# Attention units of three tiles: half-zero q and v buffers, k by pairs, and the first join in the sums' banks

## The chip, the cores and the metric

The kernel runs on one core of a Trainium2 chip. The metric is the device time of one execution in microseconds; the comparison of two kernels is made from runs on the same chip.

## What is computed

Sliding-window attention with sink positions, and then a gated feed-forward layer on all tokens.

```python
# q, k, v: (4, 8, 768, 64); n_sink 4, window 128
scores = scale * np.matmul(q, k.transpose(0, 1, 3, 2))
keep = is_sink | in_window
scores = np.where(keep, scores, -1000000000.0)
scores = scores - np.max(scores, axis=-1, keepdims=True)
a = np.exp(scores)
a = a / (np.sum(a, axis=-1, keepdims=True) + 1e-09)
attn = np.matmul(a, v)
# x: attn with heads side by side, (3072, 512)
gate = 1.0 / (1.0 + np.exp(-(x @ w_gate)))
val = x @ w_val
out = gate * val @ w_out          # w_gate, w_val: 512 x 1536; w_out: 1536 x 512
```

The weights come as 64-bit floats, in two 32-bit words each.

## The kernel before

**Attention.** Six tiles of 128 queries stand in a sequence. The table `AT` cuts the first batch into two blocks of three tiles and each of the other three batches into three blocks of two. A *unit* `u` is one head of one block, so units 0 to 15 (the first batch) have three tiles; they are the *plain* units and work in f32 without a split. The later units, of two tiles, split their operands into a rounded part and a rest and use rounded f32 (`fp32r`) products. A unit (`attend`, line 795) loads q, k (both transposed, head dimension on partitions) and v; by tile it makes scores q·k on TensorE (`qk`), masks them and takes the row maximum on VectorE (`top`), and exponentiates on ScalarE (`exp`). Then VectorE inverts the row sums (`guard`), one of POOL, ScalarE and VectorE multiplies (`norm`), TensorE transposes (`turn`), ScalarE copies (`wt`), POOL cuts the copy into two triangles (`split`), and TensorE multiplies by v (`pv`). The sink columns are gathered in `psk`.

**Plain units before.** A head has 64 dimensions. q·k takes 64 partitions of `qkT`: from `u = 4` on (`DUP`) one load brings two heads (k of a pair, q of a pair), and the second head uses the upper half. For `u < 4` each head's q and k are loaded twice, into both halves, so that the product has 128 rows, and the scale is halved. p·v of a plain unit has v as its stationary operand, 64 columns, and writes the lower or upper half of the partitions of the bank `xr`. Scores of `u < 8` go into the banks of the output sums (`OS`, named `o`), which the feed-forward part doesn't use yet; all else goes into three rotating banks `a`.

**Join.** After the eight heads of a block, `join` (line 1046) transposes `psk`, splits it (`sk`), multiplies by `vsp` (the sinks' v, from the load `v_sink`), adds the products to `xr`, and writes the sum in rounded part and rest to `XH` and `XL`. These are the operands of the feed-forward part.

**Feed-forward.** `weights` and `decode` (line 1120) load one of twelve sets of weights (set `f`: 128 columns of `w_gate`, of `w_val`, and 128 rows of `w_out`, each through one of three staging tiles `wst`) and turn the 64-bit words into a rounded part and a rest: ScalarE, VectorE and POOL share the work. For each chunk of three tiles and each `f`, `feed_part` makes 24 *up* products (`m<-XH,wgh` and so on, 384 columns), tanh on ScalarE, the gate factor on VectorE (`th`), a split (`gh`, `gl`), and nine *down* products (`o<-woh,gh`, 512 columns). `GATES` lets set 0 be decoded from `u = 2` on and the others only behind `guard` of `u = 7`.

**The order.** `Plan` holds all operations with a priority and estimates of their duration, and before anything is issued it walks through an event list and writes one fixed order for each engine: TensorE prefers attention (its priority is `u`) and fills up with up and down products; where TensorE would be idle early on, it puts in *fill* products (`m<-ident`). Each engine executes in the written order, and all loads stand in one queue, SyncE's. A tile of a pool is taken when its first operation is placed, and `plan.over` says which tiles lie under which others.

Of the kernel before, what the change touches and what calls it, by code (L numbers as in the profile page):

```python
# [32 lines left out]
DUP = 4  # L33
# [37 lines left out]
BUFS = {}  # L71
# [368 lines left out]
def kernel(  # L440
# [70 lines left out]
    def mac(cols):  # L511
        return max(cols * 13 / 12 / 2.4, 104.5) + 2.5
# [55 lines left out]
    def shared(name, n2, n3):  # L568
# [10 lines left out]
    QK = shared("qkT", 256 + 3 * KW, 384 + 4 * KW)  # L579
# [15 lines left out]
    EV = [  # L595
        WST[1][:, 768:960].rearrange("p (l d) -> p l d", d=D),
        WST[2][:, 6 * KW : 6 * KW + 192].rearrange("p (l d) -> p l d", d=D),
    ]
    early_pool = ExitStack()
    ep = early_pool.enter_context(tc.tile_pool(name="early", bufs=1))  # L600

    class Late:
# [4 lines left out]
        def tile(self, *a, **kw):  # L607
            if self.pool is None:
                early_pool.close()
                self.pool = main.enter_context(tc.tile_pool(name="late", bufs=1))  # L610
            return self.pool.tile(*a, **kw)

    late = Late()
    NQ = 3 * KW + 384
    EQ = [ep.tile([128, NQ], F32, name=f"eq{i}") for i in range(3)]
    for tag, n in (("qs", 2), ("kh", 4), ("vhl", 3)):
        for i in range(n):
            plan.over[tag, i] = {("eQ", 0), ("eQ", 1), ("eQ", 2)}
    EW = [WST[1][:, 0:768].rearrange("p (z t y x) -> p z t y x", z=1, t=3, y=2)]
    plan.over["wst", 1] = {("eW", 0), ("eV", 0)}  # L620
    plan.over["wst", 2] = {("eP", 0), ("eP", 1), ("eV", 1)}
# [146 lines left out]
    def load(u, b, h, t0, T, prev, L, vraw, qkT, plain):  # L768
# [20 lines left out]
        dma(  # L789
            u, 182.0 * L, lambda: Q.dma_start(  # L790
                out=vraw(), in_=v[b, h, :, t0 - prev : t0 - prev + L]
            ), w=[vraw],
        )

    def attend(u, b, h, t0, T, XR, XS, PSK, QKT):
# [11 lines left out]
        if early and u % 2:  # L807
            vraw = Tile(EV, None, F32, "eV", 2)
        else:
            vraw = tile([128, L, D], F32, "vraw", BUFS["vraw"])  # L810
        twice = u < DUP
        if not (plain and h % 2 and not twice):
            QKT[0] = (
                Tile(EQ, None, F32, "eQ", 3) if twice and u % 5 > 1 else part(T, QK, "qkT")
            )
        qkT = QKT[0]
        rows = slice(e, e + D) if plain and not twice else slice(0, 128)
        scale = SCALE * (0.5 if twice else 1.0)
        qT = lambda: qkT()[rows, 0:W]
        kTf = lambda: qkT()[rows, W : W + L * KW]  # L820
        load(u, b, h, t0, T, prev, L, vraw, qkT, plain)
        kk2, qq2 = [(qkT, 0), (qkT, 4)], [(qkT, 2), (qkT, 6)]
        if plain:
            pairs = ((qT, kTf),)
            qk_reads = [qkT]
        else:
            qs = tile([128, W], F32R, "qs", 2, late)
            kht = tile([128, 3 * KW], F32R, "kh", 4, late)
            klt = tile([128, 3 * KW], F32R, "kh", 4, late)
# [18 lines left out]
        for t in range(T):  # L848
            sc = Tile(OS, None, F32, "eO", 3) if early else tile([128, 512], F32, "a", BUFS["a"], ps)
# [11 lines left out]
            def top(t=t, sc=sc, first=first):  # L861
                if not first:
                    V.copy_predicated(out=sc()[:, 0:128], mask=tri, data=sc()[:, KW : KW + 128])
                V.tensor_tensor_reduce(
                    out=Pv()[:, t], in0=sc()[:, 0:KW], in1=am[min(t0 + t, 2)], op0=ALU.add,
                    op1=ALU.min, scale=-scale, scalar=3.0e38, accum_out=negm_all[:, at + t : at + t + 1],
                )

            def exp(t=t):
# [6 lines left out]
                u, [("PE", 60 + 2 * n if plain else 20 + 2 * mac(n), qk)], qk_reads, [sc, (P, t)],  # L876
                busy=0.5 if plain and not twice else 0.97,
# [84 lines left out]
        if plain:  # L962
            vhl = vht = vraw
        else:
            vht = tile([128, 3, 2 * D], F32R, "vhl", 3, late)
            vhl = lambda: vht()[:, 0:L]
            copy(u, L * D, lambda: vhl()[:, :, 0:D], vraw, [vraw], [(vht, 0)], L % 2)
            rest(
                u, L * D, lambda: vhl()[:, :, D : 2 * D], vraw, lambda: vhl()[:, :, 0:D],
                [vraw, (vht, 0)], [(vht, 1)],  # L970
            )
# [9 lines left out]
        M = D if plain else 2 * D  # L981
# [189 lines left out]

    def weights(f, prio):
        fs = slice(f * 128, f * 128 + 128)
        wres[f] = []
        for nm, w in (("g", w_gate), ("v", w_val)):
            hi = Fixed(wp.tile([128, NC, 128], F32R, name=f"w{nm}h{f}"))
            lo = Fixed(wp.tile([128, NC, 128], F32R, name=f"w{nm}l{f}"))
            decode(prio(), w[fs], hi, lo)
            wres[f] += [hi, lo]
        hi = Fixed(wp.tile([128, 1, DO], F32R, name=f"woh{f}"))  # L1180
# [8 lines left out]
    def feed(ci, g, parts):  # L1189
# [13 lines left out]
        for j, acc in enumerate(O):  # L1203
            ot = (
                part(2, QK, "qkT") if ci == len(MT) - 1 and j == 2
# [190 lines left out]
```

## Time and profile before

| | us |
|---|---|
| median of 3 runs | 776.95 |
| lowest, highest | 776.75, 776.95 |
| the profiled execution | 776.84 |
| span of the profiled execution, first to last instruction | 775.1 |
| TensorE busy | 761.6 (98%) |
| VectorE busy | 440.0 (57%) |
| ScalarE busy | 413.8 (53%) |
| POOL busy | 385.8 (50%) |

The span is the time between the first and the last instruction; the rest of the execution's time lies around it. Busy shares are means over stages that differ much, so the views below are of stretches. In a timeline a matmul's duration contains the way through the array, and following matmuls overlap; what one costs is read from start to start.

### The profile page before, as it was taken

Reading aid. Unit: us, or ns where it says so; the run is one execution under the profiler, and the core shown is the slowest. Engines: PE = TensorE matmul, PEld = TensorE weight load, DVE = VectorE, ACT = ScalarE, POOL = GpSimd, SP = SyncE. Lnnn points to the kernel's source line nnn. Section 1 sums busy time; section 2 is a strip of 40 time slices with the busy share of each in tenths; the row PEclk is TensorE's granted clock in tenths of the full one; section 3 lists DMA queues with packets and bytes.
Section 4 is the critical chain, followed back from the end, with each engine's and each line's share of the span. In section 5 each row is a group of like instructions: output and inputs, shape, how many; then the busy total and the mean of one; then the engine's idle time right before and its main releaser. Section 6 shows DMA issues by size and latency. Waiting matters only on the chain.

```text
span 775.1 us, 13683 instructions
## 1 busy us (share of the span) xinstructions
PE 761.6 (98%) x4184; PEld 689.9 (89%) x4184; DVE 440.0 (57%) x1398; ACT 413.8 (53%) x1222; POOL 385.8 (50%) x521
## 2 busy tenths in 40 slices
PE   8999999999999999999999999999999999999996
PEld 6577779999999999999999999999999999999995
DVE  5878888978885688938820578836831310100001
ACT  5776778877776676836721586735741321121111
POOL 3567658877786675825721477824731321112110
PEclk9999999999999999999999999999999999999999
DMA  6568788563433443523431235432401211121111
GB/s 174 163 220 279 247 277 261 159 190 109 128 111 103 118 122 100 145 63 124 113 89 44 93 104 147 115 96 85 114 29 49 64 51 42 47 67 59 45 41 59
DMA packets 63444, 90.05 MB, mean 116 GB/s; under 512 B 9220, under 2 KB 40964, under 8 KB 63364
## 3 DMA queue, kind: packets, MB, share of 16 engines
q1 hardware_dynamic: 63360, 89.10, 39.0%
q8 instruction: 35, 0.57, 0.3%
q14 instruction: 45, 0.37, 0.1%
q10 hardware_dynamic: 4, 0.00, 0.0%
HBM read 79.63 MB, written 9.44 MB: 115 GB/s over the span
## 4 chain that ended last, share of the span: by engine, by line
PE 94%; SPq 2%; DVE 1%; DMA 1%; POOL 1%; issue 0%; ACT 0%; DVEq 0%; POOLq 0%
PE m L493 52%; PE o L493 26%; PE a L493 16%; SPq L493 2%; DMA w<-in_v_sink_dram 1%; DVE a L493 0%; DVE P L493 0%; DVE wst L493 0%; POOL vsp L493 0%; POOL kh L493 0%; POOL wst L493 0%; POOL wt L493 0%; DVE gl L493 0%; DVE xr L493 0%; DVE kh L493 0%
## 5 line engine op out<-in xcount | busy, mean ns | idle before, releaser
L493 DVE SCALAR_TENSOR_TENSOR th<-th,m 128x384 f32<-128x384 f32 x96 | 52.9, 552 | 216.9 <-PE m L493 216.5
L493 POOL TENSOR_TENSOR gl<-th,gh 128x384 fp32r<-128x384 f32 x64 | 65.6, 1025 | 213.5 <-ACT gh L493 210.0
L493 PE MATMUL m<-XH,wgh 128*128 128x384 f32 x384 | 132.6, 345 | 0.0
L493 PE MATMUL m<-XH,wvh 128*128 128x384 f32 x384 | 131.4, 342 | 0.0
L493 POOL TENSOR_SCALAR_AFFINE_SELECT wt<-wt 128x512 fp32r<-128x512 f32 (+3 forms) x172 | 107.2, 625 | 46.5 <-DVE wt L493 33.3
L493 PE MATMUL m<-XH,wvl 128*128 128x384 f32 x384 | 129.4, 337 | 0.0
L493 PE MATMUL m<-XL,wvh 128*128 128x384 f32 x384 | 129.1, 336 | 0.0
L493 PE MATMUL m<-XH,wgl 128*128 128x384 f32 x384 | 129.0, 336 | 0.0
L493 PE MATMUL m<-XL,wgh 128*128 128x384 f32 x384 | 128.9, 336 | 0.0
L493 ACT CAST gh<-th 128x384 fp32r<-128x384 f32 x83 | 42.6, 513 | 153.3 <-DVE th L493 153.0
L493 PE MATMUL o<-woh,gh 128*128 128x512 f32 x288 | 117.1, 407 | 0.0
L493 PE MATMUL o<-woh,gl 128*128 128x512 f32 x288 | 113.5, 394 | 0.0
L493 PE MATMUL o<-wol,gh 128*128 128x512 f32 x288 | 112.7, 391 | 0.0
L493 ACT ACTIVATE P<-P,negm_all 128x132 f32<-128x132 f32 x180 | 72.5, 403 | 21.1 <-DVE negm_all L493 19.5
L493 ACT ACTIVATE th<-m 128x384 f32<-128x384 f32 x96 | 46.9, 489 | 67.0 <-PE m L493 66.2
L493 PEld LDWEIGHTS m<-XH,wvh 128*128 128x128 f32 x384 | 72.1, 188 | 4.4 <-issue 1.5
L493 PEld LDWEIGHTS m<-XH,wgh 128*128 128x128 f32 x384 | 72.2, 188 | 3.3 <-issue 2.5
L493 PEld LDWEIGHTS m<-XL,wvh 128*128 128x128 f32 x384 | 72.2, 188 | 2.7
L493 PEld LDWEIGHTS m<-XL,wgh 128*128 128x128 f32 x384 | 72.3, 188 | 0.7
L493 PEld LDWEIGHTS m<-XH,wgl 128*128 128x128 f32 x384 | 72.1, 188 | 0.0
L493 PEld LDWEIGHTS m<-XH,wvl 128*128 128x128 f32 x384 | 72.1, 188 | 0.0
L493 PEld LDWEIGHTS o<-woh,gl 128*128 128x128 f32 x288 | 54.0, 188 | 13.5 <-DVE gl L493 0.3
(135 smaller groups left out, 1445.2 us busy)
## 6 DMA issues: line engine op xcount, KB each, us to landing
wol<-wol_d SPq DMA_DIRECT2D x96, 256.0 KB, 2.7
qkT<-in_k_dram SPq DMA_DIRECT2D x100, 99.0 KB, 2.6
qkT<-in_q_dram SPq DMA_DIRECT2D x144, 64.0 KB, 2.3
wst<-in_moe_w_gate_dram SPq DMA_DIRECT2D x12, 512.0 KB, 4.9
wst<-in_moe_w_val_dram SPq DMA_DIRECT2D x12, 512.0 KB, 3.7
wst<-in_moe_w_out_dram SPq DMA_DIRECT2D x12, 512.0 KB, 4.1
out_dram<-w SPq DMA_DIRECT2D x23, 256.0 KB, 2.1
vraw<-in_v_dram SPq DMA_DIRECT2D x52, 96.0 KB, 2.2
```

Of the source, the lines that this page charges most:

```text
L493: return lambda *a, **kw: tc.keep_in_program_order(op(*a, **kw))
```

## The change

Plain units get buffers that are half zero. `QZ` holds four tiles of 128 partitions: head 0 of a pair has its q in the lower 64 partitions and zeros in the upper ones, head 1 the other way round. `VZ` does the same for v along the columns. k is loaded once by pair, both heads one above the other. q·k then multiplies 128 rows (the other head's k meets zeros), and p·v has 128 columns and writes the whole bank `xr`, where the second head's product is added to the first one's. The zeros are set once, by memsets on POOL and VectorE, since the loads write only the other half. The doubled loads, the halved scale and the early tiles `EQ` and `EV` are gone.

The scores of `u < 10` (`MORE`) instead of `u < 8` go into the sums' banks, and so do the transposes and the four products of the first join, whose priority is moved ahead by 3 (`AHEAD`). The new tiles take the room of the sets `f >= 10` (`LATE`), which are taken when all eight are free; the small tiles of the later units no longer wait for early tiles. The estimates of q·k and p·v in the plan are lower.

```diff
-DUP = 4
+AHEAD = 3.0
+MORE = 10
+LATE = 10
...
-    QK = shared("qkT", 256 + 3 * KW, 384 + 4 * KW)
+    NQ = 256 + 3 * KW
+    raw = const.tile([128, 3 * NQ], F32, name="qkT")
+    QK = [raw[:, i * NQ : i * NQ + NQ] for i in range(3)]
...
+    QZ = [[ep.tile([128, 384], F32, name=f"qz{z}{i}") for i in range(2)] for z in range(2)]
+    VZ = [[ep.tile([128, 4, 128], F32, name=f"vz{z}{i}") for i in range(2)] for z in range(2)]
+    for i in range(2):
+        for z in range(2):
+            nc.gpsimd.memset(QZ[z][i][D - z * D : 2 * D - z * D], 0.0)
+        for z in range(2):
+            nc.vector.memset(VZ[z][i][:, :, D - z * D : 2 * D - z * D], 0.0)
+    EARLY = {(f"{n}{z}", i) for n in ("qz", "vz") for z in range(2) for i in range(2)}
+    for f in range(LATE, NF):
+        for n in ("wgh", "wgl", "wvh", "wvl", "woh"):
+            plan.over[f"{n}{f}_", 0] = set(EARLY)
...
+        e = (h % 2) * D
+        vsrc = v[b, h, :, t0 - prev : t0 - prev + L]
+        if qz:
+            if h % 2 == 0:
+                dma(
+                    u, 1.5 * L * KW, lambda: Q.dma_start(
+                        out=qkT()[:, 0 : L * KW],
+                        in_=k[b, h : h + 2, :, (t0 - prev) * KW : (t0 - prev + L) * KW].rearrange(
+                            "h d n -> (h d) n"
+                        ),
+                    ), w=[qkT],
+                )
+            dma(
+                u, 0.75 * W, lambda: Q.dma_start(
+                    out=qz()[e : e + D, 0:W], in_=q[b, h, :, t0 * 128 : t0 * 128 + W]
+                ), w=[qz],
+            )
+            dma(
+                u, 182.0 * L, lambda: Q.dma_start(out=vt()[:, 0:L, e : e + D], in_=vsrc), w=[vt]
+            )
+            return
...
-            if plain and u >= DUP:
-                if h % 2 == 0:
-                    dma(
-                        u, 1.5 * n, lambda src=src, o=o, n=n, at=at: Q.dma_start(
-                            out=qkT()[:, at : at + n],
-                            in_=src[b, h : h + 2, :, o : o + n].rearrange("h d n -> (h d) n"),
-                        ), w=[(qkT, part)],
-                    )
-                continue
...
         early = u < H
-        if early and u % 2:
-            vraw = Tile(EV, None, F32, "eV", 2)
+        z = h % 2
+        qz = Tile(QZ[z], None, F32, f"qz{z}", 2) if plain else None
+        if plain:
+            vt = Tile(VZ[z], None, F32, f"vz{z}", 2)
         else:
-            vraw = tile([128, L, D], F32, "vraw", BUFS["vraw"])
-        twice = u < DUP
-        if not (plain and h % 2 and not twice):
-            QKT[0] = (
-                Tile(EQ, None, F32, "eQ", 3) if twice and u % 5 > 1 else part(T, QK, "qkT")
-            )
+            vt = tile([128, L, D], F32, "vraw", BUFS["vraw"])
+        vraw = lambda: vt()
+        if not (plain and z):
+            QKT[0] = Tile(QK, None, F32, "qkT", 3)
         qkT = QKT[0]
...
-        rows = slice(e, e + D) if plain and not twice else slice(0, 128)
-        scale = SCALE * (0.5 if twice else 1.0)
-        qT = lambda: qkT()[rows, 0:W]
-        kTf = lambda: qkT()[rows, W : W + L * KW]
-        load(u, b, h, t0, T, prev, L, vraw, qkT, plain)
+        load(u, b, h, t0, T, prev, L, vt, qkT, qz)
         kk2, qq2 = [(qkT, 0), (qkT, 4)], [(qkT, 2), (qkT, 6)]
         if plain:
-            pairs = ((qT, kTf),)
-            qk_reads = [qkT]
+            pairs = ((lambda: qz(), lambda: qkT()[:, 0 : L * KW]),)
+            qk_reads = [qkT, qz]
...
-            sc = Tile(OS, None, F32, "eO", 3) if early else tile([128, 512], F32, "a", BUFS["a"], ps)
+            sc = Tile(OS, None, F32, "eO", 3) if u < MORE else tile([128, 512], F32, "a", BUFS["a"], ps)
...
-                u, [("PE", 60 + 2 * n if plain else 20 + 2 * mac(n), qk)], qk_reads, [sc, (P, t)],
-                busy=0.5 if plain and not twice else 0.97,
+                u, [("PE", (15 + 1.7 * n if plain else 20 + 2 * mac(n)), qk)], qk_reads, [sc, (P, t)],
...
-            a = (xr()[e : e + D] if plain else acc())[:, 0 : Z * W].rearrange("p (z x) -> p z x", z=Z)
+            a = (xr if plain else acc)()[:, 0 : Z * W].rearrange("p (z x) -> p z x", z=Z)
...
-                    start=i == 0, stop=i == len(blocks) - 1, skip_group_check=True,
+                    start=i == 0 and not (plain and z), stop=i == len(blocks) - 1, skip_group_check=True,
...
-                u, [("PE", 60 + sum(2 * n for *_, n in blocks), pv)], [vht, wt], [(xr, h % 2)]
+                u, [("PE", 15 + sum(1.7 * n for *_, n in blocks), pv)], [vht, wt], [xr]
...
-        ts = tile([128, 512], F32, "a", BUFS["a"], ps)
+        first = u == H - 1
+        bank = (
+            lambda: Tile(OS, None, F32, "eO", 3) if first
+            else tile([128, 512], F32, "a", BUFS["a"], ps)
+        )
+        u -= AHEAD if first else 0
+        ts = bank()
...
-                sp = tile([128, 512], F32, "a", BUFS["a"], ps)
+                sp = bank()
...
+    def home(shape, name, f):
+
+        if f < LATE:
+            return Fixed(wp.tile(shape, F32R, name=name))
+        return tile(shape, F32R, name + "_", 1, late)
```

The order changes throughout. SyncE's queue, from the third of the early heads on, before (`w_290<-in_v_sink_dram` is the load for `vsp`, `wst` the staging of weights; `x2` counts equal loads that follow each other):

```order
L493 DMA eq_96<-in_k_dram 64x396 x2
L493 DMA eq_96<-in_q_dram 64x384 x2
L493 DMA vraw_232<-in_v_dram 128x192
L493 DMA eq_97<-in_k_dram 64x396 x2
L493 DMA eq_97<-in_q_dram 64x384 x2
L493 DMA wst_89<-in_v_dram 128x192
L493 DMA qkT<-in_k_dram 128x396
L493 DMA qkT<-in_q_dram 128x384
L493 DMA qkT<-in_k_dram 128x396
L493 DMA qkT<-in_q_dram 128x384
L493 DMA w_290<-in_v_sink_dram 96x512
L493 DMA wst_87<-in_moe_w_gate_dram 128x1024
```

and now:

```order
L495 DMA vz_101<-in_v_dram 128x3x64
L495 DMA qz_99<-in_q_dram 64x384
L495 DMA vz_103<-in_v_dram 128x3x64
L495 DMA qkT<-in_k_dram 128x396
L495 DMA vraw_217<-in_v_dram 128x128
L495 DMA vraw_226<-in_v_dram 128x128
L495 DMA qz_96<-in_q_dram 64x384
L495 DMA qz_98<-in_q_dram 64x384
L495 DMA qkT<-in_k_dram 128x396
L495 DMA vraw_288<-in_v_dram 128x128
L495 DMA w_298<-in_v_sink_dram 96x512
L495 DMA wst_87<-in_moe_w_gate_dram 128x1024
```

The v_sink load has 24 loads ahead of it before and 17 now; among them are now three v loads of later units (`vraw`).

TensorE around the first join, before (`psk` the gathered sinks, `sk,vsp` the join's products, `wt,vraw` p·v of units 8 and 7, `m<-ident` fill):

```order
L493 MATMUL a_568<-ident,psk_277 32x128 x3
L493 MATMUL m_113<-ident 128x128 x3
L493 MATMUL a_582<-wt_547,vraw_444 64x256 x2
L493 MATMUL a_582<-wt_547,vraw_444 64x128 x2
L493 MATMUL a_592<-sk_579,vsp 128x384
L493 MATMUL a_514<-wt_573,wst_89 64x256 x2
L493 MATMUL a_514<-wt_573,wst_89 64x128
L493 MATMUL m_113<-ident 128x128
L493 MATMUL a_609<-sk_579,vsp 128x384
L493 MATMUL m_113<-ident 128x128 x4
L493 MATMUL a_621<-sk_579,vsp 128x384
L493 MATMUL m_113<-ident 128x128
```

and now:

```order
L495 MATMUL o_90<-ident,psk_286 32x128 x3
L495 MATMUL a_573<-ident,wst_89 128x128 x3
L495 MATMUL m_126<-ident 128x128
L495 MATMUL a_586<-wt_556,vz_100 128x256 x2
L495 MATMUL a_586<-wt_556,vz_100 128x128 x2
L495 MATMUL o_91<-sk_581,vsp 128x384
L495 MATMUL o_92<-sk_581,vsp 128x384
L495 MATMUL o_90<-sk_581,vsp 128x384
L495 MATMUL a_604<-qkT,qz_97 128x260
L495 MATMUL o_91<-sk_581,vsp 128x384
L495 MATMUL a_514<-wt_593,vz_103 128x256 x2
L495 MATMUL a_514<-wt_593,vz_103 128x128
```

Before, the four join products stand apart, in banks `a` (the fourth behind the last row shown); now three follow each other in banks `o`, and u=7's transposes and p·v (`a_573`, `a_514`) have come behind the join's own transposes.

TensorE among the up products of set 1, before (`a<-qkT` is a q·k product of a plain unit):

```order
L493 MATMUL m_113<-XH,wgh_122 128x384
L493 MATMUL m_113<-XL,wgh_122 128x384
L493 MATMUL m_113<-XH,wgl_123 128x384
L493 MATMUL a_722<-qkT 128x260
L493 MATMUL a_729<-qkT 128x260
L493 MATMUL m_113<-XH,wgh_122 128x384
L493 MATMUL m_113<-XL,wgh_122 128x384
L493 MATMUL m_113<-XH,wgl_123 128x384
```

and now:

```order
L495 MATMUL a_705<-ident,P 128x128 x3
L495 MATMUL a_713<-qkT,qz_99 128x260
L495 MATMUL m_126<-XH,wgh_135 128x384
L495 MATMUL m_126<-XL,wgh_135 128x384
L495 MATMUL m_126<-XH,wgl_136 128x384
L495 MATMUL m_126<-XH,wgh_135 128x384
L495 MATMUL m_126<-XL,wgh_135 128x384
L495 MATMUL m_126<-XH,wgl_136 128x384
L495 MATMUL a_731<-qkT,qz_99 128x260
L495 MATMUL m_126<-XH,wgh_135 128x384
L495 MATMUL m_126<-XL,wgh_135 128x384
L495 MATMUL m_126<-XH,wgl_136 128x384
```

The two q·k products that stood side by side now stand apart, each between six up products.

## Rows read from the trace of the kernel before

**Rows 1.** The page's part 4: chain that ended last, shares by engine.
```profile
PE 94%; SPq 2%; DVE 1%; DMA 1%; POOL 1%; issue 0%; ACT 0%; DVEq 0%; POOLq 0%
```
**Rows 2.** By stretch: length, busy PE, PEld, DVE, ACT, POOL (instructions); clock, DMA share, GB/s.
```profile
8.20:48.70 40.50, 36.03 (x193) 24.68 (x191) 29.05 (x125) 30.50 (x105) 22.62 (x35) 1.00 0.67 199
48.70:150.00 101.30, 101.30 (x521) 83.42 (x521) 91.01 (x222) 78.66 (x199) 71.17 (x85) 1.00 0.76 244
150.00:768.00 618.00, 617.67 (x3445) 575.57 (x3443) 316.35 (x1032) 302.45 (x919) 290.80 (x390) 1.00 0.32 90
```
**Rows 3.** Timeline of TensorE: start, us, engine, line, operation, out<-in, rows*columns, form, count.
```profile
49.89 0.33 PE L493 MATMUL m<-XH,wvh 128*128 128x384 f32 x1
...
51.80 0.34 PE L493 MATMUL m<-XH,wgl 128*128 128x384 f32 x1
52.06 1.51 PE L493 MATMUL a<-wt,vraw 128*64 128x256 f32 x8
53.51 0.44 PE L493 MATMUL m<-XH,wvh 128*128 128x384 f32 x1
53.79 0.34 PE L493 MATMUL m<-XL,wvh 128*128 128x384 f32 x1
...
55.54 0.34 PE L493 MATMUL m<-XH,wgl 128*128 128x384 f32 x1
55.80 1.14 PE L493 MATMUL a<-qkT 64*128 64x260 f32 x4
56.88 0.44 PE L493 MATMUL m<-XH,wgh 128*128 128x384 f32 x1
57.16 0.34 PE L493 MATMUL m<-XL,wgh 128*128 128x384 f32 x1
...
62.44 0.49 PE L493 MATMUL a<-ident,P 128*128 128x128 f32 x3
62.69 0.42 PE L493 MATMUL m<-XH,wvh 128*128 128x384 f32 x1
62.95 0.34 PE L493 MATMUL m<-XL,wvh 128*128 128x384 f32 x1
```
**Rows 4.** The same timeline: a full-height q·k unit, and a join product between fills.
```profile
7.76 1.27 PE L493 MATMUL o<-qkT 128*128 128x132 f32 x6
8.87 0.38 PE L493 MATMUL m<-ident 128*128 128x128 f32 x2
...
46.08 0.44 PE L493 MATMUL a<-sk,vsp 96*128 96x384 f32 x1
46.37 0.39 PE L493 MATMUL m<-ident 128*128 128x128 f32 x2
```
**Rows 5.** TensorE's groups by shape, 48.7 to 160 us: count | busy us, mean ns | idle.
```profile
L493 PE MATMUL a<-qkT 64*128 64x260 f32 x35 | 10.8, 421 | 0.0
L493 PE MATMUL a<-wt,vraw 128*64 128x256 f32 x28 | 7.5, 392 | 0.0
L493 PE MATMUL a<-wt,vraw 128*64 128x128 f32 x28 | 4.2, 273 | 0.0
```
**Rows 6.** Timeline of TensorE: q·k of two heads together.
```profile
33.38 1.22 PE L493 MATMUL a<-qkT 64*128 64x260 f32 x6
```
**Rows 7.** Timelines of SyncE, VectorE, POOL and TensorE: steps towards the first up product.
```profile
15.09 0.43 SPq L493 DMA_DIRECT2D w<-in_v_sink_dram  x1
19.90 0.42 DVE L493 CAST vsp<-w 96x512 fp32r<-96x512 f32 x1 [0.94 <-DMA w<-in_v_sink_dram]
32.58 0.33 SPq L493 DMA_DIRECT2D wst<-in_moe_w_out_dram  x1
37.74 1.03 POOL L493 TENSOR_TENSOR wst<-wst,rs 128x396 f32<-128x396 f32 x1
48.73 0.44 PE L493 MATMUL m<-XH,wgh 128*128 128x384 f32 x1
```
**Rows 8.** Waits of VectorE and SyncE, 48.7 to 150: us in total, times, longest.
```profile
DVE th L493 <- PE m L493: 3.6, 6, 1.5
DVE P L493 <- PE a L493: 0.9, 1, 0.9
SPq L493 <- PE a L493: 13.3, 7, 4.7
```

More of the change, by code (lines that the diff above doesn't have):

```diff
@@ L594 @@
     EP = [WST[2][:, i * 3 * KW : i * 3 * KW + 3 * KW] for i in range(2)]
[L595 to L598, printed above, removed]
     early_pool = ExitStack()
-    ep = early_pool.enter_context(tc.tile_pool(name="early", bufs=1))
+    ep = early_pool.enter_context(tc.tile_pool(name="early", bufs=1, side="right"))
     class Late:
@@ L609, in tile @@
                 early_pool.close()
-                self.pool = main.enter_context(tc.tile_pool(name="late", bufs=1))
+                self.pool = ctx.enter_context(tc.tile_pool(name="late", bufs=1, side="right"))
             return self.pool.tile(*a, **kw)
     late = Late()
[L614 to L618, printed above, removed]
+    QZ = [[ep.tile([128, 384], F32, name=f"qz{z}{i}") for i in range(2)] for z in range(2)]
[9 more added lines that the diff above has]
+            plan.over[f"{n}{f}_", 0] = set(EARLY)
     EW = [WST[1][:, 0:768].rearrange("p (z t y x) -> p z t y x", z=1, t=3, y=2)]
-    plan.over["wst", 1] = {("eW", 0), ("eV", 0)}
-    plan.over["wst", 2] = {("eP", 0), ("eP", 1), ("eV", 1)}
+    plan.over["wst", 1] = {("eW", 0)}
+    plan.over["wst", 2] = {("eP", 0), ("eP", 1)}
     for i in range(3):
@@ L766, in sinks, with load @@
         )
-    def load(u, b, h, t0, T, prev, L, vraw, qkT, plain):
+    def load(u, b, h, t0, T, prev, L, vt, qkT, qz):
         W = T * 128
+        e = (h % 2) * D
[19 more added lines that the diff above has]
+            return
         for part, src, o, n in ((0, k, (t0 - prev) * KW, L * KW), (2, q, t0 * 128, W)):
             at = 0 if part else W
-            if plain and u >= DUP:
-                if h % 2 == 0:
-                    dma(
-                        u, 1.5 * n, lambda src=src, o=o, n=n, at=at: Q.dma_start(
-                            out=qkT()[:, at : at + n],
-                            in_=src[b, h : h + 2, :, o : o + n].rearrange("h d n -> (h d) n"),
-                        ), w=[(qkT, part)],
-                    )
-                continue
             for i in range(2):
@@ L788, in load @@
                 )
[L789 to L792, printed above, removed]
-        )
+        dma(u, 182.0 * L, lambda: Q.dma_start(out=vt(), in_=vsrc), w=[vt])
     def attend(u, b, h, t0, T, XR, XS, PSK, QKT):
@@ L865, in top @@
                     out=Pv()[:, t], in0=sc()[:, 0:KW], in1=am[min(t0 + t, 2)], op0=ALU.add,
-                    op1=ALU.min, scale=-scale, scalar=3.0e38, accum_out=negm_all[:, at + t : at + t + 1],
+                    op1=ALU.min, scale=-SCALE, scalar=3.0e38, accum_out=negm_all[:, at + t : at + t + 1],
                 )
@@ L962, in attend @@
         if plain:
-            vhl = vht = vraw
+            vhl = vht = vt
         else:
-            vht = tile([128, 3, 2 * D], F32R, "vhl", 3, late)
+            vht = tile([128, 3, 2 * D], F32R, "vhl", 3)
             vhl = lambda: vht()[:, 0:L]
-            copy(u, L * D, lambda: vhl()[:, :, 0:D], vraw, [vraw], [(vht, 0)], L % 2)
+            copy(u, L * D, lambda: vhl()[:, :, 0:D], vraw, [vt], [(vht, 0)], L % 2)
             rest(
                 u, L * D, lambda: vhl()[:, :, D : 2 * D], vraw, lambda: vhl()[:, :, 0:D],
-                [vraw, (vht, 0)], [(vht, 1)],
+                [vt, (vht, 0)], [(vht, 1)],
             )
@@ L980, in attend @@
         xr = XR[0]
-        M = D if plain else 2 * D
         blocks = []
@@ L1175, in weights @@
         for nm, w in (("g", w_gate), ("v", w_val)):
-            hi = Fixed(wp.tile([128, NC, 128], F32R, name=f"w{nm}h{f}"))
-            lo = Fixed(wp.tile([128, NC, 128], F32R, name=f"w{nm}l{f}"))
+            hi = home([128, NC, 128], f"w{nm}h{f}", f)
+            lo = home([128, NC, 128], f"w{nm}l{f}", f)
             decode(prio(), w[fs], hi, lo)
             wres[f] += [hi, lo]
-        hi = Fixed(wp.tile([128, 1, DO], F32R, name=f"woh{f}"))
+        hi = home([128, 1, DO], f"woh{f}", f)
         lo = tile([128, 1, DO], F32R, "wlo", BUFS["wlo"])
@@ L1204, in feed @@
             ot = (
-                part(2, QK, "qkT") if ci == len(MT) - 1 and j == 2
+                Tile(QK, None, F32, "qkT", 3) if ci == len(MT) - 1 and j == 2
                 else tile([128, DO], F32, "w2", BUFS["w2"])
```

9 lines of the change are left out of this document (5 added, 4 removed).

## Prediction

> **What bounds the kernel now.** I read the chain of work that ended last, then the engines by stretch, then TensorE's timeline, then the waits. The chain lies on TensorE for 94% of the span [rows 1]. By stretch [rows 2]: from 48.70 us on TensorE has no idle time that the profile shows (101.30 of 101.30 us, then 617.67 of 618.00), and until then 36.03 of 40.50 us, part of it fill products. So the end is set by three things: when the first up product (`m<-XH,wgh`) starts, 48.73 us [rows 7]; how long TensorE's own work is from there on; and whether TensorE has to wait on the way. The granted clock is 1.00 in all these stretches, so the clock is no term. The last 7 us (output, flag) don't change. For the third question the reader should see VectorE in 48.70 to 150: 91.01 of 101.30 us busy. That is where the 12 weight sets are decoded; after 150 it has only 316.35 of 618.00.
>
> **Switching (in TensorE's time behind 48.73).** Before, a plain q·k product uses 64 rows of the array and p·v 64 columns. Starts in the timeline give prices [rows 3]: eleven up products from 49.89 to 51.80, 0.174 each. Two q·k products with one up product on each side take 55.54 to 57.16, 1.62. Full-height f32 products [rows 4] went from 7.76 to 8.87 for 652 columns, 1.70 ns a column, so 260 columns are worth 0.443; 2 x 0.443 + 2 x 0.174 = 1.234. The group costs 0.39 more than its products. For p·v: 51.80 to 53.79 is 1.99; 768 columns x 1.70 ns + 2 x 0.174 = 1.65; 0.34 more. The extra time stands on both sides of a group (0.26 and 0.28 from start to start instead of 0.174), and it is not the data type's: three f32 transposes on the full array and the up product behind them take 62.44 to 62.95, 0.51, against 3 x 0.109 + 0.174 = 0.50 (0.109 is 128 columns at half of 1.70, one instruction each). Behind 48.73 stand 17 q·k products (34 of the 35 instructions in [rows 5]) in 13 groups and 8 units' p·v (56 instructions) in 7 groups: 13 x 0.39 + 7 x 0.34 = 7.4 us. After the change all of these use 128 rows and 128 columns, and the columns that are streamed stay the same in number (the half of zeros lies across rows and columns of the array, not along the stream). What then remains by group is 0.01 by the transposes, or 0.11 by the fill row: a join product between fills took 0.29 instead of 0.174 [rows 4]. There are some 23 groups now, since the plan no longer puts q·k products together: 0.2 to 2.6 us. I take 0.03 each, near the transposes, which have the same neighbours: 0.7. **Term: -6.7 (-7.2 to -4.8).**
>
> In [rows 6] six half-height instructions of two heads took 1.22 us while four of one head took 1.14 [rows 3]: products in different halves of the array ran partly at once. The Trainium skill, "TensorE: Matmul & The Clock Gate", section "Part 3: Packing small matmuls — row/col tiling", says the same as advice against this change: with few rows, place products in separate row groups so that they overlap, rather than run one over the whole array. By that rule the sum would lose some 0.35 us a pair; by the row it does so only where two heads stand together, which in before is ahead of 48.73, so the sum loses nothing behind it.
>
> **Start.** I follow four steps. (1) The v_sink load is issued at 15.09 [rows 7] behind 24 issues, 0.6 each; now 17 stand ahead of it, since the first four heads no longer load q and k twice. Issues alone give some 11 us; but one of the 17 is now a third v load of a later unit, whose buffer POOL frees only after u=0's norm. Between 11 and 15.1 I take 13.6. Landing took 4.8 (VectorE's cast starts at 19.90), so 18.4, 1.5 earlier, and one more score tile has been handled by then. The memsets (4 on POOL, 4 on VectorE) delay masks and first tile; bound 0.3 to 1.5 us from the widths beside POOL's 1.03 for 396 columns; they lie ahead of this wait and are hidden by it. (2) w_out of set 0 is issued at 32.58, when u=5's p·v has freed the staging tile. This moves with (1), and POOL now has u=5's select ahead of u=6's norm, and u=4's norm stands on VectorE: some 3.4 earlier. (3) u=7's norm (37.74) is planned behind that load: 34.3. (4) From that norm to the first up product there are 10.99 us. Before, the four join products stand between fills and p·v, in the rotating banks; now three follow each other in the sums' banks, and set 1's decode stands behind the join on VectorE instead of in it. Norm 1.0, gather and transposes 0.5, casts 1.4, subtraction 0.5, product and first addition 0.7, XH 0.4, XL 1.0, then p·v and q·k that stand ahead in TensorE's order 1.5, and some 1.4 for a dozen hand-overs: 8.4 us. First up product at 42.7. **Term: -6.0**; bounds -7.4 (no hand-over time) and -2.0 (only step 1 pays). One more q·k product done ahead (0.44) and two new fills behind (0.44) cancel.
>
> **VectorE's pace (a wait that takes the place of the one removed).** With the two terms TensorE would reach the end of decoding 12.7 us earlier. VectorE doesn't get faster: its decode phase starts 3.5 earlier (step 3), and it can drop its own waits for TensorE, 3.6 for the tanh factor and 0.9 for scores [rows 8]; its other 5.8 idle us are other waits, of which I count none. So it can be 3.5 to 8.0 earlier, and TensorE waits 12.7 less that: 4.7 to 9.2; zero if POOL and ACT take over enough (both have over 20 us idle in the stretch [rows 2]). I take 5.0, near the lower figure, because the plan gives TensorE other work in between. **Term: +5.0 (0 to 9.2).** After 150 VectorE is half idle, so TensorE goes on without waits, and what it has gained by then it keeps.
>
> **Sum.** The profiled execution took 776.84 us (span 775.1 and 1.7 around it); the median of the three runs is 776.95, 0.01% away. 776.84 - 6.0 - 6.7 + 5.0 = **769.1 us**, 1.0% faster. The measurement can tell some 0.2% from no change.
>
> **Rivals.**
> *TensorE never waits:* POOL, ACT and the plan's slack carry the decode. For it: no idle time on TensorE in before, with VectorE at 90%. Against: [rows 2], hardly room for 12.7 us. 776.84 - 12.7 = 764.1; with the best bounds 762.2. Chance 0.20.
> *VectorE keeps its pace:* none of its waits go, and only its earlier start counts: 776.84 - 3.5 = 773.3. For it: 91.01 of 101.30. Chance 0.12.
> *The change doesn't do what it says:* the extra time belongs to a change between f32 and rounded products, and not to the half array. Then 15 q·k and 8 p·v groups cost 8.6 instead of 7.4, and TensorE, being slower, waits less: 776.84 - 6.0 + 1.2 = 772.0. The transposes in [rows 3] speak against it, the join product in [rows 4] a little for it. Chance 0.07.
> *Slower: SyncE's queue blocks the weights.* v loads now go into four half-zero buffers that only a unit's p·v frees, and q loads into four more. They stand in the one queue ahead of weight loads, and SyncE already waited 13.3 us for TensorE in seven places in this stretch [rows 8]. Twelve of u=4 to 15's v loads and as many q loads stand so; at the mean of those seven waits, 1.9 us, eight of them ahead of a weight load are 15 us of later decoding, and TensorE waits for it: 776.84 - 12.7 + 15 = 779.1. It decides from 12.7 us on. Against it: loads have three staging tiles, so that most of such a wait is hidden. Chance 0.06.
>
> **How the numbers follow.** The forecast has 0.55. The likeliest gives the time, 769.1. Its own range, with the start's and the pace's bounds, is some 765 to 773. The range 763.5 to 774.5 takes in most of the first rival, the second and the third; it leaves out the slower case and the ends. Faster by over 0.2% (under 775.3): nearly all of the forecast, the first and third rival and most of the second, 0.87; within 0.2%: 0.06; slower: 0.07.
>
> **What would show it.** Start: the first up product near 42.7 us, the v_sink cast near 18.4, w_out's issue near 29, and three join products in a row. Switching: between up products a q·k product takes 0.44 to 0.47 from start to start, and up products beside it 0.174 to 0.19. Pace: TensorE gets idle time, some 5 us between 45 and 150, ended by VectorE, ACT or POOL at weights and tanh factors, and VectorE is above 93% busy there. The forecast is wrong if half-array groups weren't the cause (starts around q·k stay at 0.26 and 0.28), if the first up product stays behind 46, or if TensorE's idle time in that stretch is over 10 us.

## The result, and the profile after

The kernel after takes 770.31 us (median of 4 runs, 769.38 to 771.39), the kernel before 776.95 in the same comparison: ratio 0.9915, 95% interval 0.9903 to 0.9928, so 0.85% faster. The forecast was 769.1. The profiled execution took 769.95 us with a span of 768.2.

The chain of waits (the page's part 4) answers to [rows 1]. It was on TensorE for 94%; now other engines and loads hold a sixth of it:

```profile
PE 83%; DVE 5%; ACT 4%; DMA 4%; POOL 2%; issue 1%; SPq 0%; DVEq 0%; POOLq 0%; ACTq 0%
```

The stretches answer to [rows 2], with the same columns:

```profile
8.20:48.70 40.50, 37.42 (x207) 31.93 (x206) 32.51 (x141) 33.42 (x118) 25.81 (x42) 0.96 0.70 196
48.70:150.00 101.30, 98.21 (x533) 88.30 (x532) 94.53 (x232) 80.35 (x210) 77.25 (x93) 1.00 0.76 245
150.00:761.00 611.00, 610.64 (x3405) 569.00 (x3403) 311.47 (x1002) 292.37 (x886) 284.07 (x385) 1.00 0.32 89
```

The reader is to see two things: in 48.7 to 150 TensorE has 3.1 us of idle time, where it had none, and VectorE is busy for 94.53 of 101.30 us, where it was 91.01.

The steps of the start answer to [rows 7]; the rows are from the timelines of SyncE, VectorE and TensorE:

```profile
13.64 0.42 SPq L495 DMA_DIRECT2D w<-in_v_sink_dram  x1
18.73 0.41 DVE L495 CAST vsp<-w 96x512 fp32r<-96x512 f32 x1
30.25 0.33 SPq L495 DMA_DIRECT2D wst<-in_moe_w_out_dram  x1
34.45 0.57 DVE L495 TENSOR_TENSOR wst<-wst,rs 128x396 f32<-128x396 f32 x1
39.16 0.77 PE L495 MATMUL o<-sk,vsp 96*128 96x384 f32 x3
43.20 0.53 PE L495 MATMUL m<-XH,wgh 128*128 128x384 f32 x1
```

Around the plain products, TensorE's timeline answers to [rows 3]:

```profile
44.27 0.34 PE L495 MATMUL m<-XH,wgl 128*128 128x384 f32 x1
44.44 0.61 PE L495 MATMUL a<-qkT,qz 128*128 128x260 f32 x2
44.70 0.53 PE L495 MATMUL m<-XH,wvh 128*128 128x384 f32 x1
45.07 0.34 PE L495 MATMUL m<-XL,wvh 128*128 128x384 f32 x1
...
45.78 0.34 PE L495 MATMUL m<-XH,wvl 128*128 128x384 f32 x1
45.96 1.47 PE L495 MATMUL a<-wt,vz 128*128 128x256 f32 x8
47.18 0.42 PE L495 MATMUL m<-XH,wgh 128*128 128x384 f32 x1
47.44 0.34 PE L495 MATMUL m<-XL,wgh 128*128 128x384 f32 x1
```

From 44.27 to 45.07 it is 0.80 us for one q·k product (260 columns, two instructions) and the up products on its sides; by the prices of the prediction, 0.443 + 2 x 0.174 = 0.79. From 45.78 to 47.44 it is 1.66 against 1.65. The 0.39 and 0.34 a group are gone.

A wait on TensorE now looks like this (start, us; in brackets the idle time before and who ended it):

```profile
131.51 0.34 PE L495 MATMUL m<-XH,wvh 128*128 128x384 f32 x1
131.68 0.34 PE L495 MATMUL m<-XL,wvh 128*128 128x384 f32 x1
132.73 0.44 PE L495 MATMUL m<-XH,wvl 128*128 128x384 f32 x1 [0.71 <-DVE wvl L495]
```

The product waits for a part of weight set 10 that VectorE finishes at that moment. From start to start it is 1.05 us where 0.174 is normal, so 0.88 are lost; the idle time shows 0.71, since the matmul before it is drawn to its modelled end. Nine waits stand between 79 and 142 us. What a wait costs is read from starts, not from the idle column.

One sum for all kernels below: the span, less the start of the first up product, is **the rest**. For the kernel before it is 775.1 - 48.73 = 726.4 us, for the kernel after 768.2 - 43.20 = 725.0. The start brought 5.5 us and the rest only 1.4, though 7.0 us of switching are gone from it (12 groups at 0.39, one at -0.05, 7 at 0.34 from the starts in the trace of before). 726.4 - 7.0 = 719.4, so TensorE's new waits cost 5.6.

### The profile page after: what moved, and what is told of

The parts are those of the page before. It is cut to its first block, busy times and chain, and to the rows that moved or that the text cites. A ratio compares the mean times of both kernels' runs of the same rounds, so it can differ in the third digit from the quotient of the medians.

```text
span 768.2 us, 13649 instructions
## 1 busy us (share of the span) xinstructions
PE 752.6 (98%) x4174; PEld 695.2 (90%) x4174; DVE 443.3 (58%) x1398; ACT 407.1 (53%) x1211; POOL 390.0 (51%) x535
## 4 chain that ended last, share of the span: by engine, by line
PE 83%; DVE 5%; ACT 4%; DMA 4%; POOL 2%; issue 1%; SPq 0%; DVEq 0%; POOLq 0%; ACTq 0%
PE m L495 47%; PE o L495 24%; PE a L495 12%; DMA wst<-in_moe_w_out_dram 1%; DVE w L495 1%; DMA wst<-in_moe_w_gate_dram 1%; DVE a L495 1%; ACT a L495 1%; ACT wst L495 1%; DMA wst<-in_moe_w_val_dram 1%; ACT P L495 1%; POOL wst L495 1%; DMA qkT<-in_k_dram 0%; POOL wt L495 0%; DVE xr L495 0%
## 5 line engine op out<-in xcount | busy, mean ns | idle before, releaser
L495 POOL TENSOR_SCALAR_AFFINE_SELECT wt<-wt 128x512 fp32r<-128x512 f32 (+3 forms) x172 | 105.5, 614 | 44.9 <-DVE wt L495 31.3
L495 PEld LDWEIGHTS o<-woh,gl 128*128 128x128 f32 x288 | 54.0, 188 | 13.3 <-DVE gl L495 0.3
```

What stands on the lines that cost most here:

```text
L495: return lambda *a, **kw: tc.keep_in_program_order(op(*a, **kw))
```

## The experiments

Each time is a median of 4 to 11 runs in comparison with the kernel before on the same chip (776.8 to 777.2 there). Where the text says that the order is kept, the instructions of each engine stand in the same order as in the kernel after.

| kernel | time, us | span | first up product | rest |
|---|---|---|---|---|
| before | 776.95 | 775.1 | 48.73 | 726.4 |
| after | 770.31 | 768.2 | 43.20 | 725.0 |
| e1 VectorE's decode lighter | 767.36 | 765.5 | 41.18 | 724.3 |
| e2 the same in before | 776.57 | 774.6 | 47.87 | 726.7 |
| e3 half array, VectorE lighter | 785.00 | 785.1 | 54.43 | 730.7 |
| e4 half array | 785.03 | 783.2 | 52.27 | 730.9 |
| e5 no decoding of sets 1 to 11 | 762.87 | 761.7 | 41.92 | 719.8 |
| e6 short weight loads | 768.49 | 766.8 | 42.77 | 724.0 |
| e7 early table load | 769.17 | 768.1 | 42.68 | 725.4 |
| e8 join where it was | 772.20 | 771.3 | 45.70 | 725.6 |
| e9 VectorE lighter and short loads | 764.32 | 762.1 | 41.89 | 720.2 |
| e10 half array from unit 10 on | 774.77 | 772.4 | 42.07 | 730.3 |
| e11 after, again | 769.92 | 766.7 | 42.09 | 724.6 |
| e12 early table load, again | 766.49 | 764.9 | 40.47 | 724.4 |

In some of these profiled executions TensorE's granted clock fell to the lower of its two levels (0.50, which is 1.2 GHz) before 16 us: in after, e2 and e6 for a few microseconds, in e4 until about 30 us, and by the duration of its products in e3 as well. In before and the others it stayed at 1.00. So first up products are compared here between executions with the same clock: e11 is the same program as after, with its clock at 1.00, and comes to its first up product at 42.09 instead of 43.20 us. Its rest is 0.4 us shorter, so the rest moves by that much by itself.

### What makes TensorE wait

e1 and e2 take most of one decode instruction away from VectorE, in the kernel after and in the one before:

```
-  out=yi(), in0=yi(), scalar=3, in1=lw(), op0=ALU.logical_shift_left,
+  out=yi()[:, 0:64], in0=yi()[:, 0:64], scalar=3, in1=lw()[:, 0:64],
+  op0=ALU.logical_shift_left,
   op1=ALU.bitwise_or,
```

> The kernel after, in the same order, with VectorE's first decode instruction (shift and or of 512 columns, about 0.69 us, 36 times) on 64 columns instead of 512, some 0.5 us less each; the other 448 columns of every decoded weight lack their low bits. Theory (VectorE's decode paces TensorE until about 142 us): TensorE's waits between 43 and 165 us, 3.1 us that the trace shows as idle and about 2.6 inside its instructions, go away: 770.3 - 5.7 = 764.6 us (763.5 to 766). Rival (the waits belong to loads, ScalarE, GpSimd or to the order): 769 to 770.5 us, with TensorE's idle time in 48.7 to 150 us still near 3.

> The same shortened instruction in the kernel before (the low bits of 448 of 512 columns are left out). Theory: TensorE had no waits to lose there, so only the three decodes ahead of the first up product help, 0 to 1.5 us: 775.4 to 776.9 us, and the distance between the kernels grows from 6.6 us to 11 to 12.7, the sum of the start (5.5) and of the switching (7.2). Rival (VectorE paced the kernel before as well, or the switching is not worth 7): 771 to 774 us, the distance stays at 6 to 8 us.

Measured: e1 767.36, e2 776.57 (ratio 0.9993, interval 0.9984 to 1.0002). The kernel before had indeed no wait to lose, but the distance between the two kernels became 9.2 us, less than the 11 to 12.7 expected. And the theory missed in the kernel after: it became 2.9 us faster, 2.0 of it ahead of the first up product, where the clock differs too; its rest fell by 0.7 us, not by 5.7, and the stretch 48.7 to 150 has 2.3 us of idle time on TensorE still, with VectorE down to 87.40:

```profile
48.70:150.00 101.30, 99.01 (x543) 90.24 (x543) 87.40 (x239) 81.91 (x216) 78.11 (x95) 1.00 0.76 248
```

VectorE's busy time alone was not the pace. e5 asked whether it is the decoding at all. The plan keeps its order, but for sets 1 to 11 nothing of the decode is issued:

```
+        if self.mute:
+            ways = [(w[0], w[1], lambda: None, *w[3:]) for w in ways]
...
+        plan.mute = f > 0      # in weights(f); False again at its end
```

> The kernel after without the decoding of weight sets 1 to 11 (their loads and all their instructions on VectorE, ScalarE and GpSimd are left out; every set's products read set 0), TensorE's order unchanged. Theory (the 5.6 us that TensorE waits between 43 and 165 us lead back to the decoding): the waits fall below 1.5 us, 764 to 766.5 us, I take 765.5, the first up product at 42 to 43.2 us. Rival (the waits are the attention's own, scores, banks and the order): 769 to 770.5 us, idle time of TensorE in 48.7 to 150 us still near 3.

Measured: 762.87 us, a little under the range, with the first up product at 41.92, TensorE idle for 0.2 us in the stretch, and the rest 719.8:

```profile
48.70:150.00 101.30, 101.12 (x564) 93.99 (x563) 45.86 (x168) 50.22 (x162) 41.88 (x65) 1.00 0.26 74
```

That is the 719.4 of the sum above: the waits that the change brought in, 5.2 to 5.6 us, belong to the decoding.

e6 took the other thing that the decoding goes through. Each weight load needs a staging tile; there are three, and SyncE issues a load as soon as VectorE's last decode instruction has freed one. In the kernel after, from VectorE's and SyncE's timelines (the first and third row are VectorE's):

```profile
81.40 0.68 DVE L495 SCALAR_TENSOR_TENSOR w<-wst,a 128x512 int32<-128x512 int32 x1
82.14 0.33 SPq L495 DMA_DIRECT2D wst<-in_moe_w_gate_dram  x1
88.73 0.69 DVE L495 SCALAR_TENSOR_TENSOR w<-wst,a 128x512 int32<-128x512 int32 x1
89.49 0.33 SPq L495 DMA_DIRECT2D wst<-in_moe_w_gate_dram  x1
```

The tile is freed at 82.08, loaded again from 82.14, and freed at 89.42: once round in 7.35 us here, in 10 and more elsewhere.

```
-  Q.dma_start(out=words(), in_=src)
+  Q.dma_start(out=words()[:, 0:part], in_=src[:, 0:part])   # part = 64 of 512 from set 2 on
```

> The kernel after with the weight loads of sets 2 to 11 cut from 512 KB to 64 KB (seven eighths of these weights are left from an earlier load), every instruction and the order as in the kernel after. Theory (the decode goes round a loop of three staging tiles, each held some 8.9 us: load 5.3, then four instructions; a load is issued 0.1 us after its tile is free): the loop shortens by 1.5 to 2.5 us, the last weight is ready well ahead of its use, TensorE's waits fall below 2 us: 766.5 us (765 to 768). Rival (the engines that decode are the pace, loads are hidden): 769.5 to 770.5 us.

Measured: 768.49, the rest 724.0, and TensorE's idle time 2.5 us: a miss as well. TensorE's waits are all for VectorE there, and VectorE is fuller than ever:

```profile
48.70:150.00 101.30, 98.78 (x539) 89.35 (x538) 95.72 (x237) 81.02 (x214) 78.75 (x94) 1.00 0.38 113
```

With full loads and a lighter VectorE (e1), on the other hand, the longest entry among TensorE's waits is a load, that of `wol`, the rest of `w_out`, which is written out to DRAM and read back for the down products:

```profile
PE o L495 <- DMA wol<-wol_d: 1.0, 2, 0.5
PE a L495 <- DVE w L495: 0.7, 2, 0.4
PE m L495 <- POOL wvl L495: 0.4, 1, 0.4
```

So each cut seemed to have left the other limit. e9 makes both:

> The kernel after with both cuts at once: VectorE's first decode instruction on 64 of 512 columns, and the weight loads of sets 2 to 11 cut to 64 KB (the weights are wrong in both ways). Theory (two limits of nearly the same height, VectorE's queue and the round of load, decode and release in the three staging tiles; each cut alone left the other, 767.4 and 768.5 us, with TensorE's waits as long as before): TensorE's idle time in 48.7 to 150 us falls from 3 to under 1.5, 765 us (763.8 to 766.3). Rival (neither; the decode's instructions on ScalarE and GpSimd, or the fixed order of hand-overs, pace TensorE): 766.8 to 768 us with the idle time still near 3.

Measured: 764.32 us (763.82 to 764.55), 0.6 us of idle time, the rest 720.2:

```profile
48.70:150.00 101.30, 100.69 (x557) 92.61 (x556) 87.69 (x249) 83.88 (x224) 80.86 (x99) 1.00 0.40 119
```

Behind the first up product one cut is worth 0.7 or 1.0 us, hardly more than the 0.4 between two executions of after; both are worth 4.8. So two limits stand at nearly the same height: VectorE's queue, and the loads. That the round through the three staging tiles is the second one, as the theory of e6 had it, is not shown. In e6 the same two loads, an eighth as long, are still issued 7.35 us apart:

```profile
82.34 0.33 SPq L495 DMA_DIRECT2D wst<-in_moe_w_gate_dram  x1
89.69 0.37 SPq L495 DMA_DIRECT2D wst<-in_moe_w_gate_dram  x1
```

From the third `w_gate` load to the last, the mean distance is 8.51 us in e6 against 8.71 in after, not 1.5 to 2.5 us less (8.43 in e1, 8.34 in e9). What the traces do show is a slow transfer: in e1 a down product starts 4.57 us behind the issue of its `wol` load (120.34 to 124.91), with TensorE idle for it; in e9 it starts 2.87 us behind it (119.28 to 122.15) and TensorE is not idle. No run shortens the transfers without the staging loads, so the share of each stays open.

### The array

e3, e4 and e10 put the plain products back on half of the array, in the kernel after's order:

```
-  pairs = ((lambda: qz(), lambda: qkT()[:, 0 : L * KW]),)
+  pairs = ((lambda: qz()[e : e + D], lambda: qkT()[e : e + D, 0 : L * KW]),)
...
-  a = (xr if plain else acc)()[:, 0 : Z * W]
+  a = (xr()[e : e + D] if plain else acc())[:, 0 : Z * W]
...
-  lhsT=vhl()[:, l], start=i == 0 and not (plain and z)
+  lhsT=vhl()[:, l, e : e + D] if plain else vhl()[:, l], start=i == 0
```

> The kernel after with the shortened decode instruction of the first run (low bits of 448 of 512 columns left out), and its plain products put back on half of the array: q.k on the 64 rows of its head, p.v on 64 columns and partitions, the zeros not read, order and all other instructions as in the kernel after. Theory: 14 q.k groups of 0.39 and 7 p.v groups of 0.34 behind the first up product come back whole, since nothing else is waited for: 7.8 us over the first run, 772.4 us if that is at 764.6 (6.5 to 8.5 over it). Rival (the cost is that of going between f32 and rounded products, whatever part of the array): as the first run, within 1 us.

> The kernel after with its plain products put back on half of the array (q.k on 64 rows, p.v on 64 columns, the zeros not read), all else as in the kernel after. Theory: TensorE's work grows by 7.8 us, of which the waits for VectorE's decode, 5.7 us, hide a part: between 2 and 7.8 us slower, 772.3 to 778, I take 773.5; the idle time of TensorE in 48.7 to 150 us falls below 1.5 us. Rival (f32 against rounded products): 770.3 within 0.7 us.

Measured: 785.00 and 785.03 us, 17.6 over e1 and 14.7 over after, far more than either expected. Some 6 us of it are what was looked for: around the groups that stand between up or down products the starts show 0.39 and 0.34 more than the products' own time again (11 and 6 groups, 6.3 us in all), and in the kernel after 0.00. So the cost belongs to the half array, not to the data type. The rest of e3 is 6.35 longer than that of e1, of e4 5.9 longer than that of after; e4's idle time in the stretch is 1.8 us, not under 1.5. What is left lies ahead: the first up product came at 54.43 and 52.27, 13.3 later than in e1 and 9.1 later than in after. In e4 TensorE's granted clock (the third column from the end, ahead of DMA share and GB/s) stood at its lower level, 1.2 GHz, for most of 12 to 30 us:

```profile
12.00:16.00 4.00, 3.98 (x12) 2.40 (x13) 2.28 (x15) 2.16 (x13) 2.61 (x5) 0.57 0.55 145
16.00:20.00 4.00, 4.00 (x13) 2.52 (x13) 1.91 (x12) 2.66 (x12) 2.00 (x4) 0.50 0.53 168
24.00:28.00 4.00, 4.00 (x12) 2.22 (x12) 2.37 (x12) 1.97 (x8) 0.93 (x2) 0.50 0.23 59
32.00:36.00 4.00, 4.00 (x22) 2.41 (x21) 2.95 (x14) 3.37 (x13) 2.62 (x5) 1.00 0.90 241
```

e10 leaves the start alone and uses half of the array for units 10 to 15:

> The kernel after with the plain products of units 10 to 15 alone put back on half of the array; all that stands ahead of the first up product is as in the kernel after. Theory (behind the first up product half-array groups cost 0.39 and 0.34 each, and it was the start that made the whole half-array kernel 15 us slower): first up product at 42.5 to 43.5 us; 14 q.k groups and 6 p.v groups add 7.5 us of TensorE's work, of which its waits of 5.9 us hide a part: 773 us (771 to 776). Rival (more is lost behind the start than the groups show): above 778 us.

Measured: 774.77, 4.85 over e11 in the same comparison, with the first up product at 42.07 (e11: 42.09) and the rest 5.7 longer: in its range. One of its groups:

```profile
52.51 0.34 PE L495 MATMUL m<-XH,wgl 128*128 128x384 f32 x1
52.78 0.70 PE L495 MATMUL a<-qkT,qz 64*128 64x260 f32 x2
53.41 0.44 PE L495 MATMUL m<-XH,wvh 128*128 128x384 f32 x1
53.69 0.34 PE L495 MATMUL m<-XL,wvh 128*128 128x384 f32 x1
```

From 52.51 to 53.69 it is 1.18 against 0.79. The groups that can be read sum to 6.0, so TensorE's waits hid hardly any of it, where nearly two thirds of 7.5 were expected. With TensorE slower the decoding was later too: its last instruction on a staging tile starts at 144.72 us, in e11 at 138.93.

### The start

> The kernel after without the part that moves the first join: its products stand where they stood, in the rotating banks, with no priority of 3 units ahead; plain units and loads as in the kernel after. Theory (the start gains from the loads and from the join, the join some 2.6 us of it): first up product at 45 to 46.5 us, of which the decoding hides a part, 771.8 us (770.8 to 773). Rival (the start came from the loads and the full array alone): first up product at 43 to 44, 770.3 us within 0.5.

```
-  first = u == H - 1
+  first = False
```

Measured: 772.20, first up product at 45.70, both as expected. The clock stayed at 1.00 in e8, as it did in before and e11. Between those two lie 6.6 us of start, and e8 is 3.6 behind e11, so by these traces the join ahead, in the sums' banks, is worth 3.6 of the 6.6. (Beside after, whose clock fell, it looks like 2.5 of 5.5.) They are one execution each, e8's the slowest of its six and e11's the fastest of its five; the medians lie 2.3 us apart.

Comparing the starts showed something that the prediction had not seen. ScalarE's timeline of the kernel after:

```profile
7.77 1.28 ACT L495 ACT_TABLE_LOAD   x1 [7.77 <-DVE negm_all L495]
9.06 0.40 ACT L495 ACTIVATE P<-P,negm_all 128x132 f32<-128x132 f32 x1
9.47 0.49 ACT L495 ACTIVATE am<-wst 128x128 f32<-128x128 f32 x2
```

In the kernel before the table load ran at 1.60, ahead of a mask instruction that itself waited until 7.75. Now the first exponential stands first in ScalarE's order; the trace has a semaphore wait at 7.72, then the load, then the exponential, so that the load came behind the first score and held both masks back. VectorE waits 1.10 us for a mask, and TensorE 1.70 us for VectorE's first scores. e7 and e12 add one small exponential that needs nothing but a memset:

```
+    plan.op(SCALP, [("A", 10, lambda: A.activation(
+        out=hot, in_=negm_all[:, 0:1], func=AF.Exp, scale=0.0))])
```

> The kernel after with one small exponential on ScalarE right behind the two scalar loads, so that the table load (1.28 us, which ran from 7.77 to 9.05 behind the first score; in the kernel before it ran at 1.60) is done early; all orders else unchanged. Theory: TensorE's 1.70 us of idle time at 8.45 to 10.15 mostly goes, its granted clock stays at 1.00 there (it fell to 0.50 in 12 to 14 us), the first up product comes 1.3 to 2.5 us earlier, and the decoding gives a part of that back: 768.8 us (767.8 to 769.8). Rival (the start waits for the v_sink load, which is issued by its own queue): first up product at 43.2, 770.3 us.

> The kernel after, unchanged, beside the others on the same chip: 770.3 us (769.4 to 771.4); if the granted clock does not fall in the first 16 us of the profiled execution, its first up product is at 42 to 43 instead of 43.2 us.

> The kernel after with the early table load, a second time beside the kernel after: 769.2 us (767.9 to 769.8), 0.5 to 1.5 us faster than the kernel after. Rival (the difference was the chip's): equal within 0.4 us.

Measured: e7 769.17 (767.88 to 769.77), e11 769.92 (768.35 to 771.45), e12 766.49 (766.03 to 768.48). In e12 the table load is early:

```profile
1.60 1.28 ACT L495 ACT_TABLE_LOAD   x1 [1.60 <-PEq L1383]
```

Beside each other e12 is 3.4 us faster than e11, more than the 0.5 to 1.5 expected; e7, within its range, had been 1.1 faster than after's first measurement. TensorE's wait for the first scores is shorter in both (after, then e7):

```profile
10.15 2.64 PE L495 MATMUL o<-qkT,qz 128*128 128x260 f32 x8 [1.70 <-DVE negm_all L495]
10.21 2.14 PE L495 MATMUL o<-qkT,qz 128*128 128x260 f32 x8 [0.74 <-DVE negm_all L495]
```

It is 0.74 in e12 too, and 1.70 in e11, so the trace explains 0.96 us by the table load. The direction is the same both times, the size isn't settled: first up products at 42.68 and 40.47 against 43.20 and 42.09. e7's came only 0.5 earlier, where 1.3 to 2.5 were expected, although its clock stayed at 1.00: it waits 1.34 us for scores again at 31.81, which e11 and e12 don't. The profiled executions of e11 and e12 differ by 1.7 us; where the rest of the 3.4 comes from is not shown. With a ratio to the kernel before of 0.9872 (0.9857 to 0.9887) this version beats both kernels. The Trainium skill, "ScalarE: Activation LUTs", section "What ACT_TABLE_LOAD costs", gives 1283 ns for the load, as the trace does, and 1380 ns of draining beside it; the first exponential follows the load by 0.01 us in the trace of after, so the second part does not show here.

## Why the prediction was right, point by point

- **Switching, -6.7 forecast, -7.0 found.** Shown by the starts in after (0.00 a group in 17 groups) and in e3, e4 and e10 (0.39 and 0.34 again). Some details were off. The 0.03 a group that was left for it is 0.00. And of the 13 q·k groups one, at 78.5 us, holds two heads and costs -0.05: products in different halves did overlap once behind 48.73, where the text said never. The 56 p·v instructions are seven units', eight each, and not eight units'; the sum counts the seven groups, so it stands. The form differs too: a q·k product takes 0.26 from start to start and the up product behind it 0.37, and not 0.44 and 0.17; only the sum is as forecast.
- **Start, -6.0 forecast, -5.5 in the profiled execution (-6.6 in e11's).** The 1.1 us between these two executions go with the clock, which fell in after's start; "the clock is no term" held for the trace of before alone. The steps came near where they were put: v_sink's issue 13.64 (13.6), its cast 18.73 (18.4), w_out 30.25 (29), the last norm 34.45 (34.3), from there 8.75 us (8.4). Incomplete in step 1: it was the q load of unit 5 that held SyncE longest; it stood from 8.6 to 11.55, until TensorE was done with unit 1's scores, and the third v load waited only 0.5. That is why "they lie ahead of this wait and are hidden by it" fails for the masks: TensorE's wait of 1.70 us for VectorE stands among unit 1's scores, VectorE waited for a mask, and the masks came late behind the table load, which was not seen. The memsets themselves did no harm that the trace shows (the window value that the masks need is there at 6.13, in before at 6.43). e7 and e12, with the early load, are 1.1 and 3.4 us faster.
- **Pace, +5.0 forecast, +5.6 found (5.2 by e5).** The size was right, the cause half of it, so that the size is partly luck: it was worked out from VectorE's time alone. The step "VectorE doesn't get faster" made VectorE the one resource; e1 and e6 show that relieving it alone, or the loads alone, gives 0.7 and 1.0 us, and e9 that both give 4.8. The loads are the part that the step left out. VectorE did come earlier by an amount in the forecast range: its last decode instruction on a staging tile starts at 140.44 instead of 146.61, 6.2 us, within 3.5 to 8.0. Its wait for TensorE at the tanh factor, 3.6 us in [rows 8], is down to 0.2 us.
- **Rivals.** "TensorE never waits" was priced at 764.1: e5 (762.9) and e9 (764.3) show that this is what the change gives once the decoding doesn't limit it. "VectorE keeps its pace" (773.3) fell with the 6.2 us. "The change doesn't do what it says" fell with the 0.00 a group, and with e3 and e4. "SyncE's queue blocks the weights" fell: its waits for TensorE in the stretch went from 13.3 us in seven places down to this:

```profile
SPq L495 <- PE a L495: 1.6, 3, 1.1
```

- **What it said would show it** mostly did: three join products in a row, VectorE at 93%, idle time on TensorE ended by VectorE. Idle time was 3.1 and not 5; the difference is the 0.17 us by which each wait costs more than its idle time, and short waits that leave none.

## What to carry to other kernels

Filling the unused half of the array with zeros pays where single small products stand between full ones: their columns cost the same, and the 0.3 to 0.4 us around each group go. Before such a gain is booked, ask what feeds the engine that gets faster: here 12.5 us were gained and 5.6 given back to a decode that had just kept up, at two limits at once, so that relieving either one showed next to nothing. And look at what stands first on each engine: one instruction that moved up took a table load onto the path behind the first score.

## What the runs showed of the hardware

- In e4 TensorE sat idle for 1.28 us until 10.59, its clock then fell to 1.2 GHz and came back at about 30 us, though it had work all the time; its products were half-array ones and transposes. In the profiled execution of after it sat idle for 1.70 us until 10.15, and full-array products followed: 0.50 in 12 to 14 us, 0.74 in 14 to 16, 1.00 from 16 on; e6, with the same wait, ran alike (0.50, 0.64, 1.00). In e11, the same program as after, TensorE waited the same 1.70 us, but the clock stayed at 1.00 and the first up product came 1.1 us earlier. In e8, e9 and e10 the clock stayed at 1.00 behind the same wait too. So the wait alone doesn't tell whether the clock falls; why it stayed low for so much longer in e4, no run took apart. Six p·v products show the price: 2.39 us at the lower level (e4 at 20.28), 1.30 at the upper one (at 30.34).

```profile
20.28 2.39 PE L495 MATMUL a<-wt,vz 128*64 128x256 f32 x6
...
30.34 1.30 PE L495 MATMUL a<-wst,vz 128*64 128x256 f32 x6
```

- The clock in the records isn't always to be trusted: in e3 it reads 1.00 from 16 to 28 us, while six such products take 2.39 us there too (at 22.80), as at the lower level in e4.
- A table load can wait with the instruction behind it, and need not: in after it ran at 7.77 us, behind a semaphore wait that stands ahead of it and of the first exponential; in before it ran at 1.60, while the mask instruction behind it waited until 7.75; in e12 it ran at 1.60 again, ahead of the small exponential.
